# Attention on Trainium2: values and output projections as pairs of 64-row TensorE products in two passes

## The chip, the cores and the metric

The kernel runs on one core of one Trainium2 chip. The metric is the device time of one execution in microseconds. Three runs of the kernel before took 927.18, 927.53 and 929.13 us; their median is 927.53.

## What is computed

`x` has 2048 rows of 640. A layer norm of it goes two ways, through attention (32 heads of 192, keys and values from the last 512 positions of a cache) and through a gated feed-forward block. The two are multiplied and added to `x`:

```python
def _A_ref(x, k_cache, v_cache, wq, wo):
    ...
    W = min(4096, max(256, Sk // 4))
    ...
    scores = jnp.einsum("bhqd,bhkd->bhqk", q, k) * (Dh ** -0.5)
    p = _softmax(scores, axis=-1)
    o = jnp.einsum("bhqk,bhkd->bhqd", p, v)
    return (lambda x, *d: x.transpose(*d))(o, 0, 2, 1, 3).reshape(B, Sq, Hq * Dh) @ wo
...
xn = _layernorm(x, axis=-1)
s = _A_ref(xn, A_k_cache, A_v_cache, A_wq, A_wo)
g = _silu(_B_ref(xn, B_w_gate, B_w_up, B_w_down))
return x + s * g
```

Inputs and output are bfloat16; sums are kept in 32 bits.

## The kernel before

**First part (to about 178 us).** Rows are normalized in tiles of 128 and turned, so that `xnT` holds features on partitions. The feed-forward block is computed in four row blocks of 512 (`gated`, `down`) and its silu is kept in `gate`. The first row tile's gate products (`tile_gates`, L299) need `wg_sb` for 4 feature chunks, then `wu_sb`. The loads are issued at L168 to L180: `wg_sb`'s first 640 KB in one transfer on ScalarE's queue, everything else on SyncE's queue in the order of the code.

**Second part: units.** A unit `u` is a group of four heads (`g = u // 4`, eight groups) with a block of 512 rows (`b = u % 4`), 32 units in all. Four functions do its work, and each takes a pair of PSUM banks `bank[k]` (1024 columns; there are four such pairs, numbered 0 to 3):

- `scores` (L396): for one of 2 head pairs and 4 key chunks, three 64-row products for each of two heads. Head 0 of the pair has its dimensions on partitions 0 to 63, head 1 on 64 to 127, so the two products of a pair use the upper and the lower 64 rows of TensorE and different banks. ScalarE's exponential (L406) evacuates the 1024 columns to `E`.
- `queries` (L408): the projection of a later unit's queries. A product over 128 features is split in two 64-row products on the two halves of TensorE. In a first call half 0 of the rows feeds the first bank and half 1 the second, in a second call the halves are exchanged, so that the two never write one bank at a time. After the first call VectorE reads one column of each bank into `seen` (L425), so that the second call's products, which write there, wait for the first call's to be complete.
- `values` (L431): for one head, for each of four row tiles of 128, four 128-row products of 193 columns (192 values and a column of ones, whose sum is the softmax denominator), L436. Then VectorE takes the reciprocal (L441) and multiplies (L442) into `o_st`, from where `turn_out` has SyncE's queue transpose it to `oT`.
- `project` (L458): for one row tile, six 128-row products over the group's 768 features, each as 512 and 128 columns (L475). VectorE adds the result to `acc` (L482; L480 copies in the first group). In the last group `finish_rows` multiplies by `gate` (L454), adds `acc` (L455, the sum so far with `x`) and sends the rows out (L456). In group 6, POOL prepares that `acc` (L486, L487).

**Order.** It is written out by hand and kept: each engine runs its instructions in program order. The main loop (L494) takes two units at a time, 15 times. First come their scores, 8 each, on bank pairs 0 and 1 alternately, with queries of the units two later on bank pairs 2 and 3 in between. Then, for each of the two units and each of four heads, `values` is followed by a `project` of the unit two before; `order = (2, 3, 0, 1)` gives values the bank pairs 2, 0, 2, 0 and projections 3, 1, 3, 1. In the first iteration there is nothing to project yet, and the values take 2, 3, 0, 1. The tail (L523 to L545) has the scores of the last two units in runs of 6, 6 and 4 with the projections of units 28 and 29 between and behind them, then the values of units 30 and 31, then their projections. In unit 31's the 640 columns are made as two halves of 320, each finished by itself, and POOL does most of the additions of the last two units.

Of the kernel before, what the change touches and what calls it, by code (L numbers as in the profile page):

```python
# [9 lines left out]
ALU = mybir.AluOpType  # L10
BF16 = mybir.dt.bfloat16
F32 = mybir.dt.float32
# [3 lines left out]
def kernel(  # L16
# [13 lines left out]
    nc = tc.nc  # L30
    P = 128
    H2 = 64

    xf = A_x.flatten_outer_dims()
    of = out.flatten_outer_dims()
    S, D = xf.shape
    _, Hkv, Sk, DH = A_k_cache.shape
# [6 lines left out]
    KC = W // P  # L44
    TB = 512
    NB = S // TB
    TQ = TB // P
    NT = S // P
    NCD = D // P
# [3 lines left out]
    GC = GW // P  # L53
    DJ = DH // H2
# [14 lines left out]
    bank = [psum.tile([P, 2, 512], F32, name=f"bank{i}") for i in range(4)]  # L69

    def wide(i):
        return bank[i][:].rearrange("p b n -> p (b n)")
# [8 lines left out]
    gate = pers.tile([P, NT, D], BF16, name="gate")  # L81
    vbuf = pers.tile([P, 4, KC, VP], BF16, name="vbuf")
# [3 lines left out]
    wg_r = B_w_gate.rearrange("(c p) f -> p c f", p=P)  # L86
    wu_r = B_w_up.rearrange("(c p) f -> p c f", p=P)
# [6 lines left out]
    def load_wq(g, eng):  # L94
        d = grp.setdefault(g, {})
        d["wq"] = load1.tile([P, NCD, GW], BF16, name="wq_sb")
        eng.dma_start(d["wq"][:], wq_r[:, :, g * GW:(g + 1) * GW])  # L97
# [25 lines left out]
    def load_wo(g):  # L123
        d = grp[g]
        if g < NG - 1:
            d["wo"] = wo_pool.tile([P, GC, D], BF16, name="wo_sb")
        else:

            d["wo"] = load1.tile([P, GC, D], BF16, name="wo_last", tag="wq_sb")
        nc.sync.dma_start(d["wo"][:], wo_r[:, g * GC:(g + 1) * GC, :])  # L130
# [12 lines left out]
    with ExitStack() as bctx:  # L143
# [5 lines left out]
        wg_sb = wB.tile([P, NCD, F], BF16, name="wg_sb")  # L149
        wu_sb = wB.tile([P, NCD, F], BF16, name="wu_sb")  # L150
# [4 lines left out]
        def load_x(t, n):  # L155

            x = xpool.tile([P, n, D], BF16, name=f"x_sb{n}", bufs=4 if n == 1 else 2)
            nc.sync.dma_start(x[:], xf[t * P:(t + n) * P, :].rearrange("(q p) d -> p q d", p=P))
            for i in range(n):
                xt[t + i] = x[:, i, :]  # L160

        def load_f(eng, w, r, f0, f1, c0=0, c1=NCD):
            eng.dma_start(w[:, c0:c1, f0 * P:f1 * P], r[:, c0:c1, f0 * P:f1 * P])
# [3 lines left out]
        nc.vector.memset(wg_sb[:, 0, 0:2], 0.0)  # L167
        load_x(0, 1)  # L168
        load_x(1, 1)
        load_f(nc.scalar, wg_sb, wg_r, 0, 4)  # L170
        load_f(nc.sync, wu_sb, wu_r, 0, 4, 0, 3)
        load_x(2, 1)
        load_f(nc.sync, wu_sb, wu_r, 0, 4, 3, NCD)
        load_x(3, 1)
# [160 lines left out]
        k = 1  # L335
        for f in range(FT, NF):
            gated(0, f, k, norm_piece(1, f - FT))
            k = (k + 1) % 4
        for b in range(1, NB):
            for f in range(2):  # L340
                gated(b, f, k)
                k = (k + 1) % 4
            for q in range(TQ):
                down(b - 1, q, k)
                k = (k + 1) % 4
            if b == 1:
                load_x(3 * TQ, TQ)
            for f in range(2, NF):
                gated(b, f, k, norm_piece(b + 1, f - 4) if b + 1 < NB and f >= 4 else None)
                k = (k + 1) % 4  # L350
# [6 lines left out]
        for q in range(TQ):  # L357
            down(NB - 1, q, k)
            k = (k + 1) % 4
# [12 lines left out]
        for u in range(2):  # L372
            qT[u] = qpool.tile([P, 2 * DJ, TB], BF16, name="qT")
            for m in range(DJ):
                k = next(ks)
# [6 lines left out]
    acc_pool = ctx.enter_context(tc.tile_pool(name="acc_pool", bufs=1))  # L382
# [4 lines left out]
    fin = ctx.enter_context(tc.tile_pool(name="fin", bufs=2))  # L387

    acc = acc_pool.tile([P, NT, D], F32, name="acc")
    NU = NG * NB  # L390
    E = {}
    oT = {}
    seen = acc_pool.tile([P, DJ, 2], F32, name="seen")
    load_wo(0)

    def scores(u, pr, c, k):  # L396
# [32 lines left out]
    o_st = {}  # L429

    def values(u, h, k):  # L431
        e = E[u, h // 2]
        o4 = wide(k).rearrange("p (q n) -> p q n", q=TQ)
        for q in range(TQ):
            for c in range(KC):
                nc.tensor.matmul(o4[:, q, 0:DH + 1], lhsT=e[:, c, h % 2, q * P:(q + 1) * P],  # L436
                                 rhs=vbuf[:, h, c, 0:DH + 1], start=(c == 0), stop=(c == KC - 1))
        if h == 0:
            o_st[u] = o_pool.tile([P, TQ, GW], BF16, name="o_st")
        rden = small.tile([P, TQ, 1], F32, name="rden")  # L440
        nc.vector.reciprocal(rden[:], o4[:, :, DH:DH + 1])  # L441
        nc.vector.tensor_tensor(o_st[u][:, :, h * DH:(h + 1) * DH], o4[:, :, 0:DH],  # L442
                                rden[:].to_broadcast([P, TQ, DH]), ALU.mult)

    def turn_out(u):
        oT[u] = oT_pool.tile([P, GC, TB], BF16, name="oT")
        for q in range(TQ):
            nc.sync.dma_start_transpose(oT[u][:, :, q * P:(q + 1) * P], o_st[u][:, q, :])

    def finish_rows(t, d0, d1, src, add, out_eng):  # L450

        o_sb = fin.tile([P, D], F32, name="o_sb", bufs=2)[:, d0:d1]
        r_sb = gate[:, t, d0:d1]
        nc.vector.tensor_tensor(o_sb, src, r_sb, ALU.mult)  # L454
        add.tensor_tensor(r_sb, o_sb, acc[:, t, d0:d1], ALU.add)  # L455
        out_eng.dma_start(of[t * P:(t + 1) * P, d0:d1], r_sb)  # L456

    def project(u, q, k, out_eng, add=nc.vector):  # L458
        g, b = u // NB, u % NB
        wo = grp[g]["wo"]  # L460
        t = b * TQ + q
        if u == NU - 1:

            HD = D // 2
            for i in range(2):
                for cc in range(GC):
                    nc.tensor.matmul(bank[k[i]][:, 0, 0:HD],
                                     lhsT=oT[u][:, cc, q * P:(q + 1) * P],
                                     rhs=wo[:, cc, i * HD:(i + 1) * HD],
                                     start=(cc == 0), stop=(cc == GC - 1))  # L470
                finish_rows(t, i * HD, (i + 1) * HD, bank[k[i]][:, 0, 0:HD], add, out_eng[i])
            return
        for cc in range(GC):
            for d0, d1 in ((0, 512), (512, D)):
                nc.tensor.matmul(wide(k)[:, d0:d1], lhsT=oT[u][:, cc, q * P:(q + 1) * P],  # L475
                                 rhs=wo[:, cc, d0:d1], start=(cc == 0), stop=(cc == GC - 1))
        if g == NG - 1:
            finish_rows(t, 0, D, wide(k)[:, 0:D], add, out_eng)
        elif g == 0:
            nc.vector.tensor_copy(acc[:, t, :], wide(k)[:, 0:D])  # L480
        else:
            nc.vector.tensor_tensor(acc[:, t, :], wide(k)[:, 0:D], acc[:, t, :], ALU.add)  # L482
        if g == NG - 2:
            x_sb = fin.tile([P, D], BF16, name="row")
            nc.gpsimd.dma_start(x_sb[:], xf[t * P:(t + 1) * P, :])
            nc.gpsimd.tensor_tensor(acc[:, t, :], acc[:, t, :], gate[:, t, :], ALU.mult)  # L486
            nc.gpsimd.tensor_tensor(acc[:, t, :], acc[:, t, :], x_sb[:], ALU.add)  # L487

    sc = [(pr, c) for pr in range(2) for c in range(KC)]
    order = (2, 3, 0, 1)  # L490
# [3 lines left out]
    for u0 in range(0, NU - 2, 2):  # L494
        g, second = u0 // NB, u0 % NB != 0
        more = g + 1 < NG
        for u in (u0, u0 + 1):
            for i, what in enumerate(((0, 0), (1, 0), (0, 1), (1, 1), (2, 0), None, (2, 1), None)):
                scores(u, *sc[i], i % 2)
                if what is not None:  # L500
                    queries(u + 2, what[0], 2 + (what[0] + u) % 2, what[1])
        if more and not second:
            load_wq(g + 1, nc.gpsimd)
            load_keys(g + 1, nc.gpsimd)
        if more and second:
            turn_keys(g + 1)
        if not more:
            load_wo(g)
        for u in (u0, u0 + 1):
            for q in range(4):  # L510
                if u0 > 0:
                    values(u, q, order[2 * q % 4])
                    project(u - 2, q, order[(2 * q + 1) % 4], nc.sync)
                else:
                    values(u, q, order[q])
            turn_out(u)
        if more and second:
            load_values(g + 1, nc.gpsimd)
        if 0 < g < NG - 1 and not second:
            load_wo(g)  # L520


    u = NU - 2  # L523
    sc = [(v, *s) for v in (u, u + 1) for s in sc]
    for i in range(6):
        scores(*sc[i], order[i % 4])
    for q in range(2):
        project(u - 2, q, q, nc.gpsimd)
    for i in range(6, 12):
        scores(*sc[i], order[(i - 6) % 4])  # L530
    for q in range(2, 4):
        project(u - 2, q, q - 2, nc.gpsimd)
    for i in range(12, 16):
        scores(*sc[i], order[i % 4])
    for q in range(4):
        project(u - 1, q, order[q], nc.gpsimd)
    for v in (u, u + 1):
        for h in range(4):
            values(v, h, order[h])
        turn_out(v)  # L540
    for q in range(4):
        project(u, q, order[q], nc.sync, nc.gpsimd if q < 3 else nc.vector)
    for q in range(4):
        i = 2 * q % 4
        project(u + 1, q, order[i:i + 2], (nc.scalar, nc.sync), nc.gpsimd if q < 3 else nc.vector)  # L545


# [28 lines left out]
```

## Time and profile before

| | |
|---|---|
| Profiled execution | 929.13 us, of which the profile's span is 927.3 |
| TensorE (PE) busy | 914.2 us, 99% |
| VectorE (DVE) busy | 464.0 us, 50% |
| ScalarE (ACT) busy | 302.5 us, 33% |
| GpSimd (POOL) busy | 140.0 us, 15% |
| Chain that ended last | 97% TensorE: L475 22%, L420 21%, L436 19%, L402 18%, L249 10%, L261 6% |

How to read it. Times in a window or timeline are microseconds from the span's start. A row gives start, duration, engine, line, operation, what it writes and reads, shape and count; the bracket behind tells how long the engine was idle before it and what ended that. PE rows are products, PEld rows weight loads; products are pipelined, so the duration of one (247 ns for 193 columns) is longer than the distance to the next. Pieces of the chain run from one start to the next, so they give the distance. `64*128 64x512` is a product over 64 rows with 128 stationary columns and 512 moving ones. DVE, ACT, POOL and SP are VectorE, ScalarE, GpSimd and SyncE; a q behind a name is its sequencer.

### The profile page before, as it was taken

What the parts mean: (1) busy time and instruction counts of PE and PEld (TensorE: products, weight loads), DVE (VectorE), ACT (ScalarE), POOL (GpSimd) and SP (SyncE); (2) the same over time, 40 slices, a digit from 0 to 9 for tenths busy, and PEclk for the clock granted to TensorE, in tenths of its full rate; (3) what the DMA queues carried; (4) which work ended last, traced back from release to release, by engine and by line L of the source; (5) the groups of instructions that cost most, each with busy time, mean ns of one, the idle gap of its engine ahead of it and who ended that gap; (6) DMA issues with size and microseconds to landing.
All of it is one profiled execution on the core that took longest, in us unless ns stands there. A gap on an engine that the chain in (4) does not pass through costs nothing.

```text
span 927.3 us, 17975 instructions
## 1 busy us (share of the span) xinstructions
PE 914.2 (99%) x7926; PEld 547.5 (59%) x8004; DVE 464.0 (50%) x734; ACT 302.5 (33%) x333; POOL 140.0 (15%) x169
## 2 busy tenths in 40 slices
PE   8999999999999999999999999999999999999997
PEld 6445455465756565656565656566666656565665
DVE  5452522444545464545454545545554545454575
ACT  3222222255151424242423333333324242415240
POOL 1000110001002000200020011001100110174744
PEclk9999999999999999999999999999999999999999
DMA  9310330114424233332434252415251415253625
GB/s 318 80 22 8 88 86 1 43 61 86 86 53 112 77 70 69 100 88 41 97 88 102 42 96 78 111 36 103 69 115 34 108 61 101 60 121 92 102 74 126
DMA packets 162334, 76.68 MB, mean 83 GB/s; under 512 B 140976, under 2 KB 157568, under 8 KB 162256
## 3 DMA queue, kind: packets, MB, share of 16 engines
q1 hardware_dynamic: 154832, 52.72, 26.5%
q0 software_dynamic: 6192, 21.83, 8.1%
q8 instruction: 62, 1.02, 0.5%
q10 hardware_dynamic: 1232, 0.98, 0.3%
q14 instruction: 16, 0.13, 0.1%
HBM read 39.45 MB, written 2.62 MB: 45 GB/s over the span
## 4 chain that ended last, share of the span: by engine, by line
PE 97%; DMA 1%; issue 1%; POOL 0%; DVE 0%; ACT 0%; DVEq 0%
PE bank L475 22%; PE bank L420 21%; PE bank L436 19%; PE bank L402 18%; PE bank L249 10%; PE bank L261 6%; PE bank L368 1%; PE bank L299 1%; DMA wg_sb<-in_B_w_gate_dram 1%; POOL gate L455 0%; DVE o_sb L454 0%; PE bank L229 0%; DVE gate L455 0%; ACT xnT L235 0%; DVE warm L165 0%
## 5 line engine op out<-in xcount | busy, mean ns | idle before, releaser
L406 ACT ACTIVATE E<-bank 128x1024 bf16<-128x1024 f32 x256 | 255.5, 1023 | 457.0 <-PE bank L402 456.9
L420 PE MATMUL bank<-xnT,wq_sb 64*128 64x512 bf16 x1800 | 223.7, 376 | 0.0
L475 PE MATMUL bank<-wo_sb,oT 128*128 128x512 bf16 (+1 forms) x1288 | 197.9, 296 | 2.9
L402 PE MATMUL bank<-qT,kT 64*128 64x512 bf16 x1536 | 198.4, 376 | 0.0
L436 PE MATMUL bank<-vbuf,E 128*128 128x193 bf16 x2048 | 189.5, 247 | 0.0
L436 PEld LDWEIGHTS <-E 128*128 128x128 bf16 x2048 | 168.6, 98 | 18.0 <-issue 6.4
L427 DVE CAST qT<-bank 128x1024 bf16<-128x1024 f32 x90 | 110.2, 1225 | 128.5 <-PE bank L420 128.5
L475 PEld LDWEIGHTS <-oT 128*128 128x128 bf16 x1488 | 117.3, 98 | 75.8 <-issue 1.3
L420 PEld LDWEIGHTS <-wq_sb 64*128 64x128 bf16 x1800 | 93.1, 100 | 102.2
L402 PEld LDWEIGHTS <-kT 64*128 64x128 bf16 x1536 | 74.0, 94 | 89.7 <-issue 4.8
L442 DVE TENSOR_TENSOR o_st<-bank,rden 128x768 bf16<-128x768 f32 x128 | 122.5, 957 | 4.4
L482 DVE TENSOR_TENSOR acc<-bank,acc 128x640 f32<-128x640 f32 x96 | 79.2, 825 | 43.4 <-PE bank L475 43.3
L118 POOL DMA_DIRECT2D vbuf<-in_A_v_cache_dram x28 | 21.1, 753 | 306.8 <-PE bank L436 303.9
L425 DVE COPY seen<-bank 128x2 f32<-128x2 f32 x90 | 14.4, 160 | 93.8 <-PE bank L420 93.8
L441 DVE RECIPROCAL rden<-bank 128x4 f32<-128x4 f32 x128 | 23.3, 182 | 65.1 <-PE bank L436 65.1
L249 PE MATMUL bank<-xnT,wg_sb 128*128 128x512 bf16 x216 | 54.5, 379 | 0.2
L249 PE MATMUL bank<-xnT,wu_sb 128*128 128x512 bf16 x215 | 54.4, 379 | 0.3
L261 PE MATMUL bank<-wd_sb,hT 128*128 128x128 bf16 (+1 forms) x376 | 52.4, 297 | 0.4
L255 DVE TENSOR_TENSOR hT<-bank,sig 128x512 bf16<-128x512 f32 x44 | 30.3, 689 | 43.7 <-ACT sig L252 43.7
L252 ACT ACTIVATE sig<-bank 128x512 bf16<-128x512 f32 x44 | 26.3, 597 | 68.4 <-PE bank L249 63.8
L261 PEld LDWEIGHTS <-hT 128*128 128x128 bf16 x384 | 29.7, 98 | 23.1
L97 POOL DMA_DIRECT2D wq_sb<-in_A_wq_dram x7 | 6.3, 899 | 221.0 <-PE bank L420 221.0
(55 smaller groups left out, 346.4 us busy)
## 6 DMA issues: line engine op xcount, KB each, us to landing
wo_sb<-in_A_wo_dram SPq DMA_DIRECT2D x7, 960.0 KB, 5.5
wq_sb<-in_A_wq_dram POOLq DMA_DIRECT2D x7, 960.0 KB, 6.2
k_st<-in_A_k_cache_dram POOLq DMA_DIRECT2D x14, 384.0 KB, 5.4
vbuf<-in_A_v_cache_dram POOLq DMA_DIRECT2D x28, 192.0 KB, 3.4
row<-in_A_x_dram POOLq DMA_DIRECT2D x16, 160.0 KB, 2.8
oT<-o_st SPq DMA_TRANSPOSE x128, 2.6
x_sb<-in_A_x_dram SPq DMA_DIRECT2D x3, 640.0 KB, 9.9
wd_sb<-in_B_w_down_dram SPq DMA_DIRECT2D x1, 1920.0 KB, 13.5
```

The costliest lines, as they stand in the source:

```text
L249: nc.tensor.matmul(bank[k][:, half, 0:r1 - r0], lhsT=w[:, c, f * P:(f + 1) * P], rhs=xnT[:, b, c, r0:r1], start=(c == 0), stop=(c == NCD - 1))
L252: nc.scalar.activation(sig[:, 0:r1 - r0], bank[k][:, 0, 0:r1 - r0], AF.Sigmoid)
L255: nc.vector.tensor_tensor(hT[b][:, f, r0:r1], bank[k][:, 1, 0:r1 - r0], sig[:, 0:r1 - r0], ALU.mult)
L261: nc.tensor.matmul(wide(k)[:, d0:d1], lhsT=hT[b][:, f, q * P:(q + 1) * P], rhs=wd_sb[:, f, d0:d1], start=(f == 0), stop=(f == NF - 1))
L402: nc.tensor.matmul(bank[k][:, i, :], lhsT=kT[r, pr, j, c * P:(c + 1) * P], rhs=q[r, pr * DJ + j, :], start=(j == 0), stop=(j == DJ - 1))
L406: nc.scalar.activation(E[u, pr][:, c, :, :], bank[k][:], AF.Exp, scale=scale_qk)
L420: nc.tensor.matmul(bank[k][:, half, :], lhsT=wq[r, c, col:col + DJ * (P - 1) + 1:DJ], rhs=xnT[r, b, c, :], start=(c == 0 and not second), ...
L427: nc.vector.tensor_copy(qT[u][:, 2 * m:2 * m + 2, :], bank[k][:])
L436: nc.tensor.matmul(o4[:, q, 0:DH + 1], lhsT=e[:, c, h % 2, q * P:(q + 1) * P], rhs=vbuf[:, h, c, 0:DH + 1], start=(c == 0), stop=(c == KC ...
L442: nc.vector.tensor_tensor(o_st[u][:, :, h * DH:(h + 1) * DH], o4[:, :, 0:DH], rden[:].to_broadcast([P, TQ, DH]), ALU.mult)
L475: nc.tensor.matmul(wide(k)[:, d0:d1], lhsT=oT[u][:, cc, q * P:(q + 1) * P], rhs=wo[:, cc, d0:d1], start=(cc == 0), stop=(cc == GC - 1))
L482: nc.vector.tensor_tensor(acc[:, t, :], wide(k)[:, 0:D], acc[:, t, :], ALU.add)
```

## The change

Three things differ.

1. `values` and `project` make each 128-row product as two 64-row products in two passes, with the halves exchanged in the second, as `queries` does. Between the passes VectorE reads one column of each bank into `seen`. The functions are generators: `together` runs the first passes of two jobs one after the other, then the second passes with the evacuations. In the main loop one head's values go with one projection, in the first iteration and in the tail two of a kind go together. A projection's columns are two halves of 320, one to a bank. The projections of the last two units (`two=False`) keep 128 rows, with the columns in halves of 320.
2. `finish_rows` and the column-wise finish of unit 31 are gone. The multiplication and the addition of the last group's rows are always VectorE's, and the rows go out on SyncE's queue for units 28 to 30, on ScalarE's for unit 31, the very last tile's in two parts on two queues.
3. The first loads: `wg_sb`'s first three chunks on ScalarE's queue, its other two on SyncE's, and `wu_sb`'s first three behind `wg_sb`'s on ScalarE's queue.

```diff
-        load_f(nc.scalar, wg_sb, wg_r, 0, 4)
-        load_f(nc.sync, wu_sb, wu_r, 0, 4, 0, 3)
+        load_f(nc.scalar, wg_sb, wg_r, 0, 4, 0, 3)
+        load_f(nc.sync, wg_sb, wg_r, 0, 4, 3, NCD)
+        load_f(nc.scalar, wu_sb, wu_r, 0, 4, 0, 3)
...
     def values(u, h, k):
         e = E[u, h // 2]
         o4 = wide(k).rearrange("p (q n) -> p q n", q=TQ)
-        for q in range(TQ):
-            for c in range(KC):
-                nc.tensor.matmul(o4[:, q, 0:DH + 1], lhsT=e[:, c, h % 2, q * P:(q + 1) * P],
-                                 rhs=vbuf[:, h, c, 0:DH + 1], start=(c == 0), stop=(c == KC - 1))
+        for turn in range(2):
+            for qq in range(TQ // 2):
+                for c in range(KC):
+                    for i in range(2):
+                        r = slice(i * H2, (i + 1) * H2)
+                        q = (i ^ turn) * (TQ // 2) + qq
+                        nc.tensor.matmul(o4[:, q, 0:DH + 1],
+                                         lhsT=e[r, c, h % 2, q * P:(q + 1) * P],
+                                         rhs=vbuf[r, h, c, 0:DH + 1],
+                                         start=(turn == 0 and qq == 0 and c == 0),
+                                         stop=(turn == 1 and c == KC - 1), skip_group_check=True)
+            if turn == 0:
+                nc.vector.tensor_copy(seen[:, DJ, :], bank[k][:, :, 0])
+                yield
...
-    def project(u, q, k, out_eng, add=nc.vector):
+    def project(u, q, k, out_eng, two=True):
...
+        res = bank[k][:, :, 0:HD]
+        for turn in range(2 if two else 1):
+            for cc in range(GC):
+                for i in range(2):
+                    r = slice(i * H2, (i + 1) * H2) if two else slice(0, P)
+                    half = i ^ turn
+                    nc.tensor.matmul(res[:, half, :], lhsT=oT[u][r, cc, q * P:(q + 1) * P],
+                                     rhs=wo[r, cc, half * HD:(half + 1) * HD],
+                                     start=(turn == 0 and cc == 0),
+                                     stop=(cc == GC - 1 and (turn == 1 or not two)),
+                                     skip_group_check=two)
+            if two and turn == 0:
+                nc.vector.tensor_copy(seen[:, DJ + 1, :], bank[k][:, :, 0])
+                yield
         if g == NG - 1:
-            finish_rows(t, 0, D, wide(k)[:, 0:D], add, out_eng)
+            o_sb = fin.tile([P, D], F32, name="o_sb", bufs=2)
+            nc.vector.tensor_tensor(cols(o_sb[:]), res, cols(gate[:, t, :]), ALU.mult)
+            r_sb = gate[:, t, :]
+            parts = ((0, D),) if out_eng is not None else ((0, 384), (384, D))
+            for i, (d0, d1) in enumerate(parts):
+                nc.vector.tensor_tensor(r_sb[:, d0:d1], o_sb[:, d0:d1], acc[:, t, d0:d1], ALU.add)
+                eng = out_eng or (nc.scalar, nc.sync)[i]
+                eng.dma_start(of[t * P:(t + 1) * P, d0:d1], r_sb[:, d0:d1])
...
+    def together(*jobs):
+        for _ in range(2):
+            for j in jobs:
+                next(j, None)
...
-            for q in range(4):
-                if u0 > 0:
-                    values(u, q, order[2 * q % 4])
-                    project(u - 2, q, order[(2 * q + 1) % 4], nc.sync)
-                else:
-                    values(u, q, order[q])
+            if u0 > 0:
+                for q in range(4):
+                    together(values(u, q, order[2 * q % 4]),
+                             project(u - 2, q, order[(2 * q + 1) % 4], nc.sync))
+            else:
+                for q in (0, 2):
+                    together(values(u, q, order[q]), values(u, q + 1, order[q + 1]))
             turn_out(u)
...
-        project(u, q, order[q], nc.sync, nc.gpsimd if q < 3 else nc.vector)
+        together(project(u, q, order[q], nc.sync, False))
     for q in range(4):
-        i = 2 * q % 4
-        project(u + 1, q, order[i:i + 2], (nc.scalar, nc.sync), nc.gpsimd if q < 3 else nc.vector)
+        together(project(u + 1, q, order[q], nc.scalar if q < 3 else None, False))
```

More of the change, by code (lines that the diff above doesn't have):

```diff
@@ L392 @@
     oT = {}
-    seen = acc_pool.tile([P, DJ, 2], F32, name="seen")
+    seen = acc_pool.tile([P, DJ + 2, 2], F32, name="seen")
     load_wo(0)
@@ L448, in turn_out @@
             nc.sync.dma_start_transpose(oT[u][:, :, q * P:(q + 1) * P], o_st[u][:, q, :])
[L450 to L456, printed above, removed]
-    def project(u, q, k, out_eng, add=nc.vector):
+    HD = D // 2
+    def project(u, q, k, out_eng, two=True):
         g, b = u // NB, u % NB
@@ L461, in project @@
         t = b * TQ + q
[L462 to L476, printed above, removed]
-        if g == NG - 1:
-            finish_rows(t, 0, D, wide(k)[:, 0:D], add, out_eng)
+        def cols(x):
+            return x.rearrange("p (i n) -> p i n", i=2)
+        res = bank[k][:, :, 0:HD]
[11 more added lines that the diff above has]
+                nc.vector.tensor_copy(seen[:, DJ + 1, :], bank[k][:, :, 0])
+                yield
@@ L479, in project @@
         elif g == 0:
-            nc.vector.tensor_copy(acc[:, t, :], wide(k)[:, 0:D])
+            nc.vector.tensor_copy(cols(acc[:, t, :]), res)
         else:
-            nc.vector.tensor_tensor(acc[:, t, :], wide(k)[:, 0:D], acc[:, t, :], ALU.add)
+            nc.vector.tensor_tensor(cols(acc[:, t, :]), res, cols(acc[:, t, :]), ALU.add)
         if g == NG - 2:
@@ L487, in project @@
             nc.gpsimd.tensor_tensor(acc[:, t, :], acc[:, t, :], x_sb[:], ALU.add)
+        yield
+    def together(*jobs):
+        for _ in range(2):
+            for j in jobs:
+                next(j, None)
     sc = [(pr, c) for pr in range(2) for c in range(KC)]
@@ L526 @@
         scores(*sc[i], order[i % 4])
-    for q in range(2):
-        project(u - 2, q, q, nc.gpsimd)
+    together(*(project(u - 2, q, q, nc.sync) for q in range(2)))
     for i in range(6, 12):
         scores(*sc[i], order[(i - 6) % 4])
-    for q in range(2, 4):
-        project(u - 2, q, q - 2, nc.gpsimd)
+    together(*(project(u - 2, q, q - 2, nc.sync) for q in range(2, 4)))
     for i in range(12, 16):
         scores(*sc[i], order[i % 4])
-    for q in range(4):
-        project(u - 1, q, order[q], nc.gpsimd)
+    for q in (0, 2):
+        together(*(project(u - 1, q + i, order[q + i], nc.sync) for i in range(2)))
     for v in (u, u + 1):
-        for h in range(4):
-            values(v, h, order[h])
+        for h in (0, 2):
+            together(*(values(v, h + i, order[h + i]) for i in range(2)))
         turn_out(v)
     for q in range(4):
-        project(u, q, order[q], nc.sync, nc.gpsimd if q < 3 else nc.vector)
+        together(project(u, q, order[q], nc.sync, False))
     for q in range(4):
-        i = 2 * q % 4
-        project(u + 1, q, order[i:i + 2], (nc.scalar, nc.sync), nc.gpsimd if q < 3 else nc.vector)
+        together(project(u + 1, q, order[q], nc.scalar if q < 3 else None, False))
 _INS = ['A_x', 'A_k_cache', 'A_v_cache', 'A_wq', 'A_wo', 'B_x', 'B_w_gate', 'B_w_up', 'B_w_down']
```

## The prediction

> **What bounds the kernel now.** I read the page's busy shares first, then its chain, then the groups by line, then narrow windows of the chain and of the timeline.
>
> ```profile
> PE 914.2 (99%) x7926; PEld 547.5 (59%) x8004; DVE 464.0 (50%) x734; ACT 302.5 (33%) x333; POOL 140.0 (15%) x169
> PE 97%; DMA 1%; issue 1%; POOL 0%; DVE 0%; ACT 0%; DVEq 0%
> L436 PE MATMUL bank<-vbuf,E 128*128 128x193 bf16 x2048 | 189.5, 247 | 0.0
> L442 DVE TENSOR_TENSOR o_st<-bank,rden 128x768 bf16<-128x768 f32 x128 | 122.5, 957 | 4.4
> L425 DVE COPY seen<-bank 128x2 f32<-128x2 f32 x90 | 14.4, 160 | 93.8 <-PE bank L420 93.8
> ```
>
> TensorE is the bound: 97% of the chain, no idle time before L436, the granted clock at 9 tenths or more in every slice. VectorE is half idle. So a gain must come from TensorE taking less time for the same products, and any wait that TensorE receives is paid in full. What the present products cost is read from the chain in narrow windows, where each piece runs from start to start:
>
> ```profile
> 235.35 0.65 PE bank L402 x6
> 236.00 1.44 PE bank L436 x16
> ...
> 247.96 1.33 PE bank L436 x16
> ```
> ```profile
> 259.81 0.76 PE bank L402 x6
> 260.57 1.08 PE bank L420 x10
> 261.65 0.65 PE bank L402 x6
> ```
>
> Sixteen value products take 1.33 us, 83.3 ns each. The first sixteen after scores take 1.44: passing from 64-row to 128-row products costs 0.11 us, and the way back costs the same (six score products take 0.76 after projections, 0.65 after queries). Ten 64-row query products of 512 columns take 1.08 us, 216 ns for a pair; a 128-row product of 512 columns takes as much (L249: 10.74 us for 50, of which the chain lists 49). A pair on two tiles is therefore worth one full product, no more. The chain also has 1.63 us for the 12 products of a projection, 0.272 us for 640 columns.
>
> **Products.** Values become 16 pairs of 193 columns a head, 16 x 83.3 = 1.33 us as before; a projection becomes 12 pairs of 320 columns, 12 x 136 = 1.63 us as before. No row has a narrow 64-row pair, so its cost is bounded. Below: not under the 83.3 ns of the full product, since at 512 columns pair and product are equal, unless a pair sheds fixed cost. Above: the two weight loads of a pair come one after the other. Nearest row: in a projection a 128-column product with its own weight load passes in about 56 ns (272 less 216), so a load needs 56 ns or less and two in sequence up to 112, which is 29 ns more a pair, 2048 x 29 = +59 us. I take 83.3 because a pair's two loads start 7 ns apart in the trace and last 92 to 96 ns each (L402), no longer than the 96 to 100 of L436's full loads: they run side by side. Both ends stay for the range.
>
> The Trainium skill, "TensorE: Matmul & The Clock Gate", section "LDWEIGHTS (loading the stationary operand)", speaks against the change: a load takes about columns / 1.2 ns whatever the number of rows, so 107 ns for 128 columns, and the change doubles the loads. As an estimate from that page, two loads side by side would make a value pair 107 instead of 83.3 ns, +48 us over 2048 pairs. The 56 ns row above contradicts its 107 as a spacing, so I do not count it.
>
> **Mode changes.** Stage by stage the program passes between 64 and 128 rows 36 times; after it, twice. 29 of those removed lie before the tail: 29 x 0.11 = **-3.2 us**.
>
> **Steady cycle (values of one head with one projection).** Order now: values first pass A0 (0.67), projection first pass B0 (0.82), A1 (0.67), B1 (0.82), 2.96 us in all, as before. A1 must wait for the `seen` copy after A0, and VectorE takes that copy only after the work of the cycle before. These rows give the delays:
>
> ```profile
> 250.76 1.50 PE L436 MATMUL bank<-vbuf,E 128*128 128x193 bf16 x16
> 252.30 0.18 DVE L441 RECIPROCAL rden<-bank 128x4 f32<-128x4 f32 x1 [0.51 <-PE bank L436]
> 252.51 0.96 DVE L442 TENSOR_TENSOR o_st<-bank,rden 128x768 bf16<-128x768 f32 x1
> ...
> 253.93 0.82 DVE L480 COPY acc<-bank 128x640 f32<-128x640 f32 x1 [0.46 <-PE bank L475]
> ```
> ```profile
> 893.06 0.82 DVE L454 TENSOR_TENSOR o_sb<-bank,gate 128x640 f32<-128x640 f32 x1 [2.02 <-PE bank L475]
> 893.99 0.83 DVE L455 TENSOR_TENSOR gate<-o_sb,acc 128x640 bf16<-128x640 f32 x1
> 894.73 0.82 DVE L454 TENSOR_TENSOR o_sb<-bank,gate 128x640 f32<-128x640 f32 x1
> ...
> 899.93 0.96 DVE L442 TENSOR_TENSOR o_st<-bank,rden 128x768 bf16<-128x768 f32 x1
> ...
> 900.81 0.17 DVE L441 RECIPROCAL rden<-bank 128x4 f32<-128x4 f32 x1
> ```
>
> The first fence shows a head's end: the reciprocal starts 0.28 after the last product starts (252.02 to 252.30), the multiplication 0.217 after it. The second shows VectorE without idle time: a next, independent instruction starts 0.74 us after a 640-wide one and 0.875 after the 768-wide one; a dependent one (L454 to L455) 0.93 after. From A1's start: 0.59 to its last product, 0.28, 0.217, then 0.875 (multiplication), 0.74 (accumulation), 0.16 (`seen`), 0.05 back to TensorE (two start-up rows, the end of an `xn` part to the next weight load): 2.92 us against 2.96. Slack 0.04 us: the cycle just holds. Cost **0**; below, nothing can be gained, since TensorE is the longer side; above, if each of the five hand-overs takes 0.03 more, 0.11 us in 98 cycles (7 in each of 14 stages), +11 us. I take zero, the nearest rows' sum.
>
> **Boundary to scores.** Here is a real loss. The first score after a stage writes bank 0, which the last head's values used; the first score waits for VectorE there. Before, that head ended 1.63 us ahead of the stage's end, and its evacuation (0.28 + 0.217 + 0.957) was through. Now A1 ends only 0.82 ahead: from A1's start 0.59 + 0.28 + 0.217 + 0.957 + 0.05 = 2.10, while B1 ends at 1.48. TensorE stands 0.62 us; behind it queue all scores and queries, and nothing else of use. Thirteen boundaries x 0.62 = 8.1; after the first stage (values only, B1 ends at 1.33) 0.77. The boundary to the tail has none, its first scores take banks 2 and 3. **+8.8 us**.
>
> **First stage.** Values pair with values, a cycle of 2.67 us. VectorE's loop: 0.87 + 0.217 + 0.875 + 0.217 + 0.875 + 0.16 + 0.05 = 3.27. Three cycles wait 0.60: **+1.8 us**.
>
> **Tail.** It has six mode changes fewer, -0.6. The finishing addition is now always on VectorE, so a pair of projections costs it 2 x (0.93 + 0.74) = 3.34 us against 3.26 of TensorE, and the next pair's `seen` stands behind it. Unit 29's second pair: last addition's successor 1.02 + 0.93 + 0.74 + 0.93 + 0.74 = 4.36 after A1's start, `seen` and hand-over 4.57, due at 3.26: +1.31. Values of unit 30 the same, due at 2.96: +1.61. Four value pairs follow, three waits of 0.60: +1.8. The transposes' 0.41 us wait (the idle time at 908.76) shrinks by about 0.3, as values last longer. Other pairs lie behind 4 or 6 scores and are covered. At the end eight multiplications and additions run at 1.67 on VectorE instead of POOL's share: from the first product 1.84 + 7 x 1.67 + 0.93 + 0.47 + 0.43 = 15.4 us; before, 14.7 (909.26 to 923.98): +0.6. Rounded by following the banks through, **+4.0 us**. Moving output transfers from POOL's to SP's queue puts them ahead of `turn_out`, which waits for later work anyway: 0.
>
> **Start.** The wait for `wg_sb` ends at 8.08; products could begin at about 6.5, when `xnT` is there. A smaller first piece lands earlier, but `wu_sb` moves behind it on ScalarE's queue: 640 KB took that queue until 8.03, so 768 KB takes until about 9.2, and the `wu_sb` products begin at 9.21 now. The head start is waited away: **0**, bounds -1.6 (all idle time gone) and +0.7. The further issue on ScalarE (0.45) delays its table load, covered by 1.27 us of idle time.
>
> **Sum**: -3.2 + 0 + 8.8 + 1.8 + 4.0 + 0 = +11.4 us. The profiled execution took 929.13 us (span 927.3 and 1.8 around it) and so would take 940.5. The three runs' median is 927.53, the profiled one being their slowest; against the median I forecast **938.9 us**, 1.2% slower, own range 934 to 943.
>
> **Rivals.**
> 1. *VectorE's loop is the bound*: if hand-overs make the loop 0.1 us longer than 2.96, 98 cycles add 9.8: 948.7. For it: only 0.04 us of slack. Against: the sum uses measured starts.
> 2. *Narrow pairs are slower*, by weight loads or by issue (four instructions in 83 ns, where the quickest present stretch issues two in 56): 8 to 29 ns on 2048 pairs, 955 to 998. If the tiles do not run side by side at all, which would mean that the change does not do what it says, 2048 x 83 = +170, 1109. Against: loads of a query pair overlap.
> 3. *Faster*: narrow pairs shed fixed cost. Place: the 2048 pairs of values. The sign turns at 11.4 / 2048 = 5.6 ns, a pair under 77.7 ns; at 75 ns the time is 922. Against: 512-wide pairs and products both take 216 ns, and 193 of 512 columns already make 81.4 of the 83.3.
>
> **Chances.** Forecast 0.62, loop bound 0.13, slower pairs 0.11, faster pairs 0.10, and 0.04 that small savings cancel the waits. The predicted time is the forecast's. The range 934 to 951 takes in the forecast and the first rival; outside lie the pairs, either way, 0.2. A measurement here tells 0.2% (1.9 us) from no change: faster 0.10, same 0.04, slower 0.86.
>
> **What would show it.** Right: value and projection stages without mode gaps; VectorE named as releaser of TensorE at the first score of 14 stages, about 0.6 us each; `seen` as releaser in the first stage and in the tail, 0.6 to 1.6 us each; sixteen value pairs spaced 83 ns; no or tiny waits in the steady cycles; the first up-projection product near 9.2. Wrong: waits at each second pass (rival 1), value pairs spaced over 90 ns (rival 2) or under 78 (rival 3), or no wait at the first scores.

## The result, and the profile after

The changed kernel took 942.66 us (median of 4 runs, 942.01 to 943.09) against 927.61 for the kernel before, a ratio of 1.016 (95% interval 1.014 to 1.018): 1.6% slower. The forecast was 938.9 us in a range of 934 to 951. Between the two profiled executions the span grew from 927.3 to 941.1 us, 13.8 us. (The medians differ by 15.05; the profiled execution before was its kernel's slowest.)

From the page of the kernel after, the busy shares, the chain, two groups of products and one of the added copies:

```profile
PE 920.3 (98%) x11474; PEld 630.1 (67%) x11492; DVE 486.7 (52%) x984; ACT 302.7 (32%) x333; POOL 125.7 (13%) x152
PE 93%; DVE 5%; DMA 1%; issue 1%; DVEq 0%; ACT 0%; ACTq 0%
L443 PE MATMUL bank<-vbuf,E 64*128 64x193 bf16 x4096 | 212.6, 243 | 3.9 <-DVE seen L450 3.9
L403 PE MATMUL bank<-qT,kT 64*128 64x512 bf16 x1536 | 201.3, 376 | 6.7 <-DVE o_st L456 6.5
L488 DVE COPY seen<-bank 128x2 f32<-128x2 f32 x120 | 19.1, 159 | 52.7 <-PE bank L482 51.4
```

The chain, 97% TensorE before, now holds 5% of VectorE, and two groups of products have idle time ahead of them. Do not read the loss off the idle column: it counts only the time in which no product was in flight, and a product's recorded 240 to 376 ns cover part of every wait. The view of the waits of TensorE alone, in total, times and longest:

```profile
PE bank L403 <- DVE o_st L456: 6.5, 14, 0.6
PE bank L443 <- DVE seen L450: 3.9, 7, 1.4
...
PE bank L482 <- DVE seen L488: 1.1, 1, 1.1
```

Fourteen, seven and one: the boundaries to scores, the first stage with the tail, and unit 29's second pair, as forecast. What each costs is read from the chain; its pieces here run from the recorded end of one product to that of the next, which gives the same distances as starts do while products of one kind follow each other. The steady cycles and the way into them, in the second stage:

```profile
237.88 0.43 PE bank L403 x4
238.31 0.67 PE bank L443 x16
238.97 0.00 issue
238.97 0.99 PE bank L482 x12
239.97 0.67 PE bank L443 x16
240.63 0.82 PE bank L482 x12
241.45 0.67 PE bank L443 x16
242.11 0.81 PE bank L482 x12
```

Sixteen narrow products, eight pairs, take 0.67 us: 83.3 ns a pair, exactly the full product's distance. Twelve projection products take 0.82, as worked out. No extra time lies between scores and values any more (0.67, not 0.67 and 0.11). But the first projection pass of the stage takes 0.99 instead of 0.82, which the prediction did not have. The rows of the timeline at this place show VectorE still casting queries out of the bank that the projection writes:

```profile
237.70 1.23 DVE L428 CAST qT<-bank 128x1024 bf16<-128x1024 f32 x1 [2.21 <-PE bank L421]
238.13 0.84 PE L443 MATMUL bank<-vbuf,E 64*128 64x193 bf16 x16
238.97 0.99 PE L482 MATMUL bank<-wo_sb,oT 64*128 64x320 bf16 x12
```

The projection starts 0.04 us after the cast's end. From the second product of the last values pair to it are 0.245 us, where 0.064 is usual: 0.18 us of waiting. And the end of that stage:

```profile
259.89 0.81 PE bank L482 x12
260.71 0.68 PE bank L443 x16
261.39 0.02 issue
261.41 0.19 DVE rden L455
261.61 0.02 issue
261.63 0.97 DVE o_st L456
262.60 0.04 issue
262.64 0.82 PE bank L403 x6
```

The chain has the last second pass of values from 260.71; the last projection pass would be through at 262.19 (0.67 and 0.82 later), but the chain leaves TensorE and goes over VectorE: reciprocal and multiplication of the last head. From the second product of the last projection pair to the first score are 0.747 us, where 0.116 is usual from such a pair to the next work: the score starts at 262.64 instead of 262.01, 0.63 us of waiting. (The expectations below have 0.61 and 0.16 us for these two waits. They take off the whole distance between pairs, 0.136 and 0.083, where from a pair's second product to the next first one only 0.116 and 0.064 lie.)

Stretch by stretch, from marks in both traces, the 13.8 us are: -0.2 until the first score (an accident of the execution profiled before, see Start below); +2.5 for the first stage with its boundary; +7.7 for the 13 periods from there to the last boundary (47.82 against 47.23 us each); under 0.1 for the last period; +3.9 for the tail up to the first projection of unit 30; under 0.1 from there on.

### The profile page after: what moved, and what is told of

It reads as the page before. It is cut to its first block, busy times and chain, and to the rows that moved or that the text cites. A ratio compares the mean times of both kernels' runs of the same rounds, so it can differ in the third digit from the quotient of the medians.

```text
span 941.1 us, 25256 instructions
## 1 busy us (share of the span) xinstructions
PE 920.3 (98%) x11474; PEld 630.1 (67%) x11492; DVE 486.7 (52%) x984; ACT 302.7 (32%) x333; POOL 125.7 (13%) x152
## 4 chain that ended last, share of the span: by engine, by line
PE 93%; DVE 5%; DMA 1%; issue 1%; DVEq 0%; ACT 0%; ACTq 0%
PE bank L421 21%; PE bank L482 20%; PE bank L403 18%; PE bank L443 17%; PE bank L250 10%; PE bank L262 5%; DVE o_st L456 3%; PE bank L369 1%; DVE o_sb L492 1%; DVE gate L497 1%; PE bank L300 1%; DMA wu_sb<-in_B_w_up_dram 1%; DVE rden L455 0%; PE bank L230 0%; DVE seen L450 0%
## 5 line engine op out<-in xcount | busy, mean ns | idle before, releaser
L421 PE MATMUL bank<-xnT,wq_sb 64*128 64x512 bf16 x1800 | 226.4, 376 | 0.0
L482 PE MATMUL bank<-wo_sb,oT 64*128 64x320 bf16 x2688 | 222.8, 296 | 0.0
L443 PE MATMUL bank<-vbuf,E 64*128 64x193 bf16 x4096 | 212.6, 243 | 3.9 <-DVE seen L450 3.9
L403 PE MATMUL bank<-qT,kT 64*128 64x512 bf16 x1536 | 201.3, 376 | 6.7 <-DVE o_st L456 6.5
L443 PEld LDWEIGHTS <-E 64*128 64x128 bf16 x4096 | 186.6, 94 | 15.6 <-issue 5.3
L482 PEld LDWEIGHTS <-oT 64*128 64x128 bf16 (+1 forms) x2976 | 166.2, 94 | 30.1 <-issue 3.9
L421 PEld LDWEIGHTS <-wq_sb 64*128 64x128 bf16 x1800 | 106.4, 100 | 88.9
L403 PEld LDWEIGHTS <-kT 64*128 64x128 bf16 x1536 | 86.4, 94 | 85.0 <-issue 10.5
L426 DVE COPY seen<-bank 128x2 f32<-128x2 f32 x90 | 14.4, 160 | 97.2 <-PE bank L421 97.2
L253 ACT ACTIVATE sig<-bank 128x512 bf16<-128x512 f32 x44 | 26.3, 597 | 68.4 <-PE bank L250 65.3
L488 DVE COPY seen<-bank 128x2 f32<-128x2 f32 x120 | 19.1, 159 | 52.7 <-PE bank L482 51.4
```

Of the source, the lines that this page charges most:

```text
L253: nc.scalar.activation(sig[:, 0:r1 - r0], bank[k][:, 0, 0:r1 - r0], AF.Sigmoid)
L403: nc.tensor.matmul(bank[k][:, i, :], lhsT=kT[r, pr, j, c * P:(c + 1) * P], rhs=q[r, pr * DJ + j, :], start=(j == 0), stop=(j == DJ - 1))
L421: nc.tensor.matmul(bank[k][:, half, :], lhsT=wq[r, c, col:col + DJ * (P - 1) + 1:DJ], rhs=xnT[r, b, c, :], start=(c == 0 and not second), ...
L443: nc.tensor.matmul(o4[:, q, 0:DH + 1], lhsT=e[r, c, h % 2, q * P:(q + 1) * P], rhs=vbuf[r, h, c, 0:DH + 1], start=(turn == 0 and qq == 0 a ...
L482: nc.tensor.matmul(res[:, half, :], lhsT=oT[u][r, cc, q * P:(q + 1) * P], rhs=wo[r, cc, half * HD:(half + 1) * HD], start=(turn == 0 and c ...
```

## Experiments

Theory: the narrow pairs cost what the full products cost, the mode changes (passages between 64-row and 128-row products) are gained, and TensorE pays for four kinds of waits on VectorE. Rivals: the pairs themselves are slower; the loss is all in the first stage and the tail; VectorE has room.

### The wait at the first score

```diff
-                scores(u, *sc[i], i % 2)
+                ahead = i in (0,)
+                if not ahead:
+                    scores(u, *sc[i], i % 2)
                 if what is not None:
                     queries(u + 2, what[0], 2 + (what[0] + u) % 2, what[1])
+                if ahead:
+                    scores(u, *sc[i], i % 2)
```

> The first query projection of each unit is put ahead of the unit's first score, nothing else. Theory (TensorE stands 0.61 us before the first score of each stage, for the last head's evacuation): the 1.08 us of query products cover the wait, 13 x 0.61 + 0.76 = 8.7 us less than the changed kernel's 942.7, so 934.0; VectorE is no longer named before the first score. Rival (the loss is spread over the narrow pairs themselves): 942 to 943.

934.87 us (934.41 to 935.13), 7.8 less than the changed kernel. The chain at the same boundary:

```profile
261.01 0.67 PE bank L443 x16
261.67 0.82 PE bank L482 x12
262.49 1.08 PE bank L421 x10
263.57 1.29 PE bank L403 x12
```

Ten query products follow the projection with no time between, and twelve score products then run through. The waits of L403 on `o_st` are gone from TensorE's list. The period of a stage falls from 47.82 to 47.19 us, by 0.63. Thirteen of these and the 0.78 after the first stage make 9.0 of the change's 15 us for this wait alone (8.7 were expected). Of this about 1.1 came back, 0.9 of it at one place: in the first unit two scores now come close together before ScalarE has loaded its table for the exponential, and the third score waits for the first's evacuation.

### The wait at the first projection

The same edit with `i in (6,)`: the last query projection goes ahead of the score before it.

> The last query projection of each unit is put ahead of the score before it, so that two scores instead of one stand between it and the values. Theory (the first projection of a stage waits 0.16 us for the bank that VectorE is still casting queries from): 0.65 us more cover, 15 x 0.16 = 2.4 us less than 942.7, so 940.2. Rival (that wait is hidden by something else that is late, such as the seen copy queued behind the cast): 942 to 943.

948.91 us, 6.2 more instead of 2.4 less; a miss. The chain in the middle of a score stage shows why:

```profile
225.27 0.66 PE bank L403 x6
225.93 0.02 issue
225.96 1.03 ACT E L407
226.99 0.04 issue
227.03 0.82 PE bank L403 x6
```

The wait at the first projection did go: no distance there is longer than the products' own. But the unit's last two scores now stand next to the following unit's first, three in a row on two bank pairs, and the third waits 0.62 us for ScalarE's exponential of the first. That happens 15 times, +9.4; with 15 waits of 0.18 gone, -2.7, and a first score that comes 0.5 earlier in this trace (177.57 against 178.11), it is the 6.2 measured. The theory of the wait at the first projection holds; my edit had its own fault, which goes if the first query is moved as well (below).

### Only the main loop

The kernel before, with the paired functions in the main loop from the second iteration on; first loads, first stage and tail as before.

```diff
                 if u0 > 0:
-                    values(u, q, order[2 * q % 4])
-                    project(u - 2, q, order[(2 * q + 1) % 4], nc.sync)
+                    together(values2(u, q, order[2 * q % 4]),
+                             project2(u - 2, q, order[(2 * q + 1) % 4], nc.sync))
```

> The pairs of 64-row products only in the main loop from its second iteration on; first loads, first stage and tail as before. Theory: 13 stage periods longer by 0.61 + 0.16 - 0.18 = 0.59 us, 7.7 us over before, 935.3; the first stage and the tail make up the rest of the change's loss. Rival (the main loop is even, the loss lies in the tail and the first stage): 927 to 929. Rival (narrow pairs are slower everywhere): over 940.

935.90 us (935.25 to 936.03): 8.4 over the kernel before, measured beside it (927.45), where 7.7 was expected. (Its trace has one pause of 0.3 us at 717.59 that the changed kernel's has not, and does not tell the cause.) TensorE's waits are 13 on `o_st` and none on `seen`. So somewhat more than half of the loss lies in the main loop, and the rest, 6.8 us, in the first loads, the first stage and the tail. No run takes these three apart; what they cost is read from traces.

### How much room VectorE has

```diff
             nc.vector.tensor_tensor(cols(acc[:, t, :]), res, cols(acc[:, t, :]), ALU.add)
+            nc.vector.tensor_copy(extra[:], bank[k][:, 0, 0:128])
```

> The changed kernel with one more VectorE copy (128 columns from PSUM, result unused) behind each of the 96 accumulations of groups 1 to 6, worth 128 / 0.96 + 73 = 0.206 us of VectorE's time by the spacing of its other rows. Theory (the steady cycle holds with only 0.055 us of slack, the rest of VectorE's half-idle time being of no use): 84 cycles wait 0.15 us, 12.7 us more, 955.4. Rival (VectorE, 52% busy, has room): 942.7. Rival (no slack at all): 84 x 0.206 = 17.3 more, 960.

954.28 us, 11.6 more, on a VectorE that is busy 53% of the span. The chain of a steady stage:

```profile
341.04 0.81 PE bank L444 x16
341.85 0.82 PE bank L483 x12
342.66 0.67 PE bank L444 x16
343.33 0.82 PE bank L483 x12
344.14 0.81 PE bank L444 x16
```

Every other values pass now takes 0.81 instead of 0.67: the second pass, or what is ahead of it, waits 0.14 us, 84 times (11.8 us). VectorE's rows of the same stretch show the loop without a gap from the multiplication to the `seen` copies:

```profile
342.10 0.96 DVE L457 TENSOR_TENSOR o_st<-bank,rden 128x768 bf16<-128x768 f32 x1
342.98 0.81 DVE L504 TENSOR_TENSOR acc<-bank,acc 128x640 f32<-128x640 f32 x1
343.71 0.28 DVE L505 COPY extra<-bank 128x128 f32<-128x128 f32 x1
343.91 0.15 DVE L451 COPY seen<-bank 128x2 f32<-128x2 f32 x1
344.18 0.16 DVE L489 COPY seen<-bank 128x2 f32<-128x2 f32 x1
```

0.20 us were added (343.71 to 343.91), 0.14 were paid: the steady cycle had about 0.06 us of slack. The engine's idle half is of no use to it, because it lies before the reciprocal (0.65 us in this run), where VectorE has to wait for the values pass that it is to read.

### Both queries ahead: with pairs and without

The main-loop kernel of above, and the kernel before, each with `ahead = u0 > 0 and i in (0, 6)` in the edit shown first.

> The kernel with pairs only in the main loop, with each unit's first query projection ahead of its first score and the last one ahead of the score before it (from the second iteration on). Theory: both waits of a stage (0.61 at its end, 0.16 at its start) are covered, 13 x 0.61 + 14 x 0.16 = 10.2 us less than the 935.9 of that kernel, and what stays of the change is the gain of the mode changes, 28 x 0.1 = 2.8 us under before: 924.6 to 925.7. Rival (pairs cost something that the waits hid, or the reordering makes ScalarE late as in the last-query experiment): 927 or more.

924.80 us (924.31 to 924.96), ratio to before 0.9959 (0.9946 to 0.9972): **0.4% under the kernel before**, and 11.1 us under the main-loop kernel, where 13 waits of 0.63 and 14 of 0.18 make 10.7. The chain at a boundary has products and nothing else:

```profile
257.59 0.81 PE bank L534 x12
258.40 1.08 PE bank L420 x10
259.49 1.29 PE bank L402 x12
```

> The kernel before with the same two queries moved ahead, products left as 128-row ones. Theory: it has neither wait, so nothing is covered, 927.5 as before; the distance to the pairs' kernel with this order is then the mode changes alone, 2.8 us. Rival (the order itself is what helps): 925.

927.50 us (ratio 0.9995, 0.9986 to 1.0003): the order alone changes nothing that can be measured. So the 2.7 us between these two kernels are the pairs' own gain, 28 mode changes fewer at 0.1 us.

### Many mode changes

The faster kernel again, with projections as pairs and values as full products.

```diff
-                    together(values2(u, q, order[2 * q % 4]),
-                             project2(u - 2, q, order[(2 * q + 1) % 4], nc.sync))
+                    job = project2(u - 2, q, order[(2 * q + 1) % 4], nc.sync)
+                    next(job)
+                    values(u, q, order[2 * q % 4])
+                    next(job)
```

> As the pairs' kernel with the queries moved ahead, but values stay 128-row products and only projections are pairs: first pass, values of the head, second pass. Theory (each passage between 64 and 128 rows costs 0.1 us of TensorE, and there are now two a head, 16 a stage instead of none): 14 x 16 x 0.1 = 22.4 us over that kernel, 947 to 948. Rival (a change of mode costs only where scores meet values, something else being late there): 925 to 927.

951.11 us, 26.3 more than the faster kernel, 3 to 4 above what was expected. Its chain:

```profile
245.42 1.44 PE bank L436 x16
246.86 1.74 PE bank L534 x24
248.60 1.44 PE bank L436 x16
250.04 1.74 PE bank L534 x24
```

Values of a head take 1.44 (1.33 alone), the two projection passes 1.74 (1.63 alone): 0.11 us at each passage, as between scores and values before. 224 passages make 24.0, by 0.096 before the first product and 0.011 before the second. The rest is the stage's first projection pass, which now comes earlier than the bank it needs: 0.19 us, 14 times, or 2.6. (The two profiled spans differ by 26.5.)

## Why the prediction was right, and where it fell short

- **Products**: right. Pairs of 193 columns stand 83.3 ns apart, pairs of 320 take 0.136 us, and L443's loads are recorded with 92 to 96 ns like L402's. The estimate from the Trainium skill, "TensorE: Matmul & The Clock Gate", section "LDWEIGHTS (loading the stationary operand)", was 107 ns a pair with two loads side by side. The runs do not show it: the measurement decides, 83.3.
- **Mode changes**: right, 0.107 us each. The 2.7 us between the two kernels with both queries ahead, and the 26.3 in the other direction, are its two checks. Of the prediction's 36 before and 2 after, five go in the tail and not six; that is 0.1 us.
- **Steady cycle**: right, no wait; the slack of 0.04 was 0.06.
- **Boundary to scores**: right, 0.63 (forecast 0.62) thirteen times and 0.78 (0.77) once.
- **First stage**: right: three waits of 0.60 as forecast. From `seen`'s end to TensorE's next product the rows have 0.052 us, the hand-over assumed. With the boundary, and a wait at the entry that was not forecast (next), the first stage is 2.5 longer.
- **Entry to a stage**: the step that failed, because I did not make it. The prediction asked of each stage which wait comes at its end and in its cycles, not whether the first projection's bank was free. VectorE is casting the last queries from bank 3 (237.70 to 238.93 in the second stage) and the projection wants it. Before, the whole of a head's values, 1.33 us, lay in front of it; now only a first pass of 0.67. 15 waits of 0.18 are 2.7 us, the largest part of the error of 3.8.
- **Tail**: right in place, and +3.8 of +4.0 with the end included. That the total is so close is partly luck: the terms that the prediction lists add up to 4.4, and its step from there to 4.0 is not worked out. The waits are 1.32 and 1.61 (forecast 1.31 and 1.61) and three of 0.60. One score more than expected waited about 0.4, for a bank whose evacuation stood behind an addition that took 1.28 us while POOL was at work, instead of 0.83. That POOL's work is the reason was not tried.
- **End**: the finishing on VectorE took 15.3 us as worked out (15.4), 0.6 longer than before, but the span did not get longer by it: from VectorE's last addition to the end are 2.7 us instead of 3.3. Before, POOL's closing drain ended at 926.55, 0.7 us after SyncE had finished; after, POOL has nothing to do there and follows SyncE at once. That this is the cause was read from the traces and not tried.
- **Start**: mis-sized, about +0.8 us instead of 0. The prediction took 8.08 as the start of the first gate products; that was a late landing of `wg_sb` in the one execution it had. In the four other traces with the loads unchanged these products start at 6.2 to 6.5 with a wait for the load of at most 0.2 us, the `wu_sb` products at 7.4 to 7.7, and the first scores at 176.8 to 177.2. With the changed loads (the changed kernel and the three experiments built on it) the first gate products start at 6.0 to 6.3 and the `wu_sb` products only at 8.0 to 9.0 (forecast: near 9.2); the second part's first product starts at 177.5 to 178.1. So there was hardly a head start to win, and the `wu_sb` products come later. No run has the loads alone; up to there the kernels' code differs in the loads alone.
- The entry's 2.7 and the start's 0.8 are 3.5 of the error of 3.8 against the median.

Of the rivals, the loop as bound was near: 0.06 us decided. Slower pairs and faster pairs are both refuted by the 0.67 us of sixteen narrow products.

## What to carry to other kernels

Splitting a stage's work into two interleaved passes moves every evacuation towards the end of its stage; ask at both ends of the stage, and for each buffer, what is now released later and what is needed earlier. A small gain on the bounding engine (2.7 us of mode changes here) is kept only if the order around it gives those waits something to stand behind: with the pairs in the main loop alone, two query projections moved by one place turned +0.9% into -0.4%. (The whole change with both moved was not run.) Room on a second engine is the slack of the loop that the first one waits for, not its idle share. And a term that is read from one execution needs a second one: the late load at the start was that execution's own.

## What the runs showed of the hardware

- A passage between 64-row and 128-row products costs 0.096 to 0.098 us before the first product and 0.011 more before the second, in both directions and whatever the products, 36 times before the change and 224 times in the last experiment.
- Two 64-row products with different halves pass in the time of one at 193, 320 and 512 columns (83, 136 and 216 ns), with two weight loads a pair.
- VectorE starts its next independent instruction about 0.08 us before the recorded end of the last (0.73 for a 0.81 us accumulation, 0.875 for 0.957). Adding up durations would have found the steady cycle 0.1 us too long for TensorE and forecast a wait that is not there.
